# A transformer block on one core: the attention stage's order of work, written out in the kernel instead of searched for while building

## The chip, the cores and the metric

The kernel runs on one core of one Trainium2 chip. The metric is device time in microseconds (us); the median of three runs of the kernel before is 2465.46 us (2460.82 to 2471.02). A profile of one further execution, which took 2466.89 us, is read below.

The engines are named as the profile names them: PE (TensorE, matmuls; PEld are its weight loads), DVE (VectorE), ACT (ScalarE), POOL (GpSimd) and SP (SyncE, which issues nearly all DMAs). Each runs its own list of instructions in the order in which the kernel was built.

## The reference

```python
mod = (silu(c) @ w_mod).reshape(1, 6, 1, -1)
sa, ca, ga, sb, cb, gb = (mod[:, i] for i in range(6))
h = layernorm(x) * (1 + ca) + sa
x = x + ga * attention(h, wqkv, wo)        # 32 heads of 18, softmax(q k^T / sqrt(18)) v, then @ wo
h = layernorm(x) * (1 + cb) + sb
x = x + gb * (silu(h @ w1) @ w2)           # 576 -> 4608 -> 576
return x
```

The sequence has 2048 rows of 576 numbers, in float32. Matmuls are done in a reduced float32 form, with operands split into a high and a low part, so that one product of the reference is two or three products here.

## The kernel before, in words

The rows are four blocks of 512 queries. Attention is done block by block, and in each block for eight quads of four heads. The work beside it differs: beside the first block's attention run the remaining q and k projections, beside that of block b + 1 the output projection and the whole MLP of block b. The last block's projection and MLP come alone at the end. So the program has a start (projections, up to about 156 us), four attention stages, here stage 0 to stage 3, and a tail from about 2192 us.

In a stage PE is given five kinds of work, in an order that one list fixes:

- **A slot** ("s" in the list, function `slots`, L311): two matmuls of half the array's height, one of scores (`psa`, L978), whose row maximum DVE takes (`mx`, L980), and one of scores once more, transposed (`psb`, L1061), whose exponential ACT takes (`pt`, L1063). `psb` has two PSUM banks, `psa` three in stage 0 and two later. There are 2048 slots; the scores for the maximum run 38 pairs of slots ahead of the others.
- **A unit** (a digit n stands for n units, function `values`, L374): eight matmul rows in the profile, `psv` at L1071, which multiply a finished piece of `pt` with the values. The array is used in another tiling here (quarters by columns), so that going in and out is a change of mode.
- **A filler item** ("f", function `item`, L441): the next piece of the projections or the MLP, mostly two or three pairs of half-height matmuls at L734. Items come in a fixed sequence, `FILL`.
- **A turn** is a place inside a group of such items: the halves of the array swap their two PSUM banks. PE's next matmul waits there for a small ACT instruction (L741), which itself waits for the last matmul of the first halves. ACT works in order, so that it comes behind the exponentials.
- **Rows** ("x", function `rows`): short full-height transposes at a quad's end (`pst`, `pso`).

Each PE step is followed by work of other engines. Where these instructions and the DMA issues on SP stand in their lists is decided by `Sim`, a model of the core inside the kernel: it keeps a clock per engine, and pushes each following instruction when the model says that its input is there. So the list of PE steps also fixes the order on ACT, DVE, POOL and SP.

Before the change the list comes from `search` (L519), a beam search over this model at build time. It keeps 24 states per level and 4 units in a row at most; `choices` (L489) lets the filler run at most 24 slots ahead of or behind an even pace, holds a quad's rows back until they are due, and adds a unit only when its exponentials are within 200 of the model's nanoseconds of being done. The list found is then played once more, with instructions emitted (L1868 to L1877):

```python
    order, best = sim.search()
    sim = Sim(FILL, ENDS, LOADS)
    sim.hT = HT
    with tc.manual_schedule():
        sim.real = Emit()
        sim.skip()
        for what in order:
            assert sim.act(what)
```

What is left of `FILL` when the list ends is emitted ahead of the last block's tail.

Of the kernel before, what the change touches and what calls it, by code (L numbers as in the profile page):

```python
# [31 lines left out]
NQUAD = H // 4  # L32
# [16 lines left out]
EML = 4  # L49
GB = 6  # L50
MB = 4
END = -4
END0 = 40
LP0 = 1000
LP = 8000
PB = 10
# [13 lines left out]
MOVE = {"k": 4 * 608, "q": 4 * 608, "v": 2300, "m": 320, "raw": 645, "w": 1700, "ws": 1480, "x": 780, "qk": 1640, "rawqk": 1280}  # L70
COLD = 3000
SWITCH = {("half", "values"): 115, ("values", "half"): 250, ("half", "full"): 195, ("full", "half"): 95, ("full", "values"): 95, ("values", "full"): 143}
RUN = 4
ROWS = 1400
AHEAD = 24
BEAM = 24
GRAIN = 300
PHI = 60
ACT_, DVE_, GPS_, SP_ = range(4)


def f(ap):
# [30 lines left out]
class Sim:  # L113


    def __init__(self, fill, ends, loads):
        self.fill, self.ends, self.loads = fill, ends + ends[-1:], loads
        self.sums = [sum(it.cost for it in fill[a:b]) for a, b in zip([0] + ends, ends)] + [1]
        self.real = None
        self.t = self.n = self.w = self.dma = 0  # L120
        self.mode = "half"
        self.free = [0] * 4
        self.queue = [[] for _ in range(4)]
        self.rings = {"f": [0] * 2, "a": [0] * 3, "b": [0] * 2, "v": [0]}
        self.head = {"f": 0, "a": 0, "b": 0, "v": 0}
        self.keys = {k: 0 for k in [("mr", 0), ("Q", 0), ("Q", 1), ("V", 0), ("kb", 0)] + [("ka", n) for n in range(6)]}
        self.held = {}
        self.exps = {}
        self.now = 2 * LEAD
        self.total = NQB * NQUAD * 32  # L130
        self.p = 0
        self.pend = []
        self.later = []
        self.pos = 0
        self.done = 0
        self.span = 2 * LEAD, NQUAD * 64 - END0
        self.block = 0
        self.path = None

    def clone(self):  # L140
        s = Sim.__new__(Sim)
        s.__dict__.update(self.__dict__)
        s.free = self.free[:]
        s.queue = [q[:] for q in self.queue]
        s.rings = {k: v[:] for k, v in self.rings.items()}
        s.head = dict(self.head)
        s.keys = dict(self.keys)
        s.held = dict(self.held)
        s.exps = dict(self.exps)
        s.pend = self.pend[:]  # L150
        s.later = self.later[:]
        return s

    def push(self, chain, i, ready):
        self.n += 1
# [114 lines left out]
    def key(self, k):  # L270
        return self.keys.get(k)

    def ahead(self):
        if self.pos >= self.ends[self.block]:
            return 0
        a, n = self.span
        return self.now - (a + n * self.done / self.sums[self.block])

    def more(self):
        return self.now < 2 * (self.total + LEAD)  # L280

    def over(self):
        return not (self.more() or self.pend or self.later)

    def skip(self):

        while self.pos < self.ends[self.block]:
            it = self.fill[self.pos]
            if it.cost and it.fn is not None:
                return True  # L290
            if it.keys:
                if any(self.keys.get(k) is None for k in it.keys):
                    return True
            if it.opens and not self.reopen():
                return False
            self.pos += 1
            self.done += it.cost
            if self.real and it.fn:
                it.fn()
            for delay, chain in it.chains:  # L300
                self.push(chain, 0, self.t + delay)
            self.set(it.sets, self.t)
        return True
# [112 lines left out]
    def rows(self):  # L416

        _, _, kind, i = self.later[0]
        key = ("ms", i) if kind == "m" else ("ov", i)
        at, rel = self.known(lambda: self.key(key)), self.known(lambda: self.when("a"))  # L420
        if at is None or rel is None:
            return False
        b, qd = divmod(i, NQUAD)
        self.later.pop(0)
        rel = max(at, rel)
        slot = ("r", "a", self.take("a")[0])
        if kind == "m":
            self.work(110, "full", rel)
            e = self.real.max_b(i) if self.real else (None, None)
            self.push((Op(DVE_, 270, e[0], (slot,)), Op(SP_, ROWS, e[1], (("k", ("mr", i)),), MOVE["m"])), 0, self.t + 150)  # L430
            return True
        self.work(440, "full", rel)
        e = self.real.out_b(i) if self.real else (None,) * 6
        chain = [Op(DVE_, 252, e[0])] + [Op(DVE_, 225, e[1 + n], (slot,) if n == NST - 1 else ()) for n in range(NST)]
        if qd == NQUAD - 1:
            chain.append(Op(GPS_, 650, e[5], (("k", ("post", b)),)))
            self.block = b + 1
            self.done = 0
            self.span = self.now, NQUAD * 64 - END
        self.push(tuple(chain), 0, self.t + 150)  # L440
        return True  # L441

    def item(self):
# [21 lines left out]
            self.push(chain, 0, self.t + delay)  # L465
        self.set(it.sets, self.t + 500)
        self.pos += 1
        self.done += it.cost
        return True

    def act(self, what):
        ok = {"s": self.slots, "f": self.item, "x": self.rows}[what]() if what != "v" and not isinstance(what, int) else self.values(what)
        return ok and self.skip()

    def ready(self):

        n = 0
        for kid in self.pend[:RUN]:
            c, at = self.exps.get(kid, (0, 0))
            if kid[0] != self.pend[0][0] or c < 4 or at > self.t + 200:  # L480
                break
            n += 1
        return n

    def choices(self):
        self.advance()
        work = self.pos < self.ends[self.block]
        ahead = self.ahead()
        out = []  # L489
        if self.later:  # L490
            due, last = self.later[0][:2]
            can = self.can_rows()
            if can and self.now >= last:
                return ["x"]
            if can and (self.now >= due or not self.more()):
                out.append("x")
            if not can and self.now >= last:
                return ["f"]
        n = self.ready()
        if n:  # L500
            out.append(n)
        elif self.pend and (not self.more() or self.p >= PB):
            out.append(1)
        room = self.p + (self.now % 2 == 0) <= PB
        if self.more() and room and (ahead < AHEAD or not work):
            out.append("s")
        if work and (ahead > -AHEAD or not self.more()):
            out.append("f")
        if not out:
            out = ["f"] if work else ["s"]  # L510
        return out

    def search(self):

        self.skip()
        levels = {0: [self]}
        heap = [0]
        best = None
        while heap:  # L519
            lv = heappop(heap)  # L520
            states = levels.pop(lv)
            states.sort(key=lambda s: s.t + PHI * len(s.pend))
            seen, kept = {}, 0
            for s in states:
                sig = s.now, s.pos, len(s.pend), len(s.later)
                if seen.get(sig, 0) >= 2:
                    continue
                seen[sig] = seen.get(sig, 0) + 1
                kept += 1
                if kept > BEAM:  # L530
                    break
                if s.over():
                    rest = sum(it.cost for it in self.fill[s.pos:])
                    if best is None or s.t + rest < best[0]:
                        best = s.t + rest, s
                    continue
                made = []
                for what in s.choices() + [None]:
                    if what is None:
                        if made or s.pos >= s.ends[s.block]:  # L540
                            break
                        what = "f"
                    c = s.clone()
                    if c.act(what):
                        c.path = s.path, what
                        made.append(c)
                for c in made:
                    k = c.w // GRAIN
                    if k not in levels:
                        levels[k] = []  # L550
                        heappush(heap, k)
                    levels[k].append(c)
        out, p = [], best[1].path
        while p:
            out.append(p[1])
            p = p[0]
        return out[::-1], best


class Task:  # L560
# [96 lines left out]
def tile_adaln_block(ctx: ExitStack, tc: tile.TileContext, x, wqkv, wo, w1, w2, c, wfirst, wcol, out):  # L657
# [1209 lines left out]

    sim = Sim(FILL, ENDS, LOADS)  # L1868
    sim.hT = HT
    order, best = sim.search()  # L1870
    sim = Sim(FILL, ENDS, LOADS)
    sim.hT = HT
    with tc.manual_schedule():
        sim.real = Emit()
        sim.skip()
        for what in order:
            assert sim.act(what)  # L1877
        sim.t = 10 ** 9
        sim.advance()
    state["tail"] = True  # L1880
# [53 lines left out]
```

## Time and profile before

| | |
|---|---|
| median of three runs | 2465.46 us |
| profiled execution | 2466.89 us |
| its span, first to last instruction | 2465.1 us |
| PE busy | 2391.9 us, 97% |
| DVE busy | 1777.0 us, 72% |
| ACT busy | 1491.2 us, 60% |
| POOL busy | 581.9 us, 24% |
| mean granted TensorE clock | 0.991 |

Times in the trace are counted from the span's start. "Busy" of PE runs to the end of each matmul as modelled, and matmuls overlap, so that two halves that run side by side show about 0.39 us each while the next pair begins 0.23 us after them. What PE achieves is therefore read from the distance between starts. A row of waits says how long an engine was idle before the instructions named, and whose end released it.

### The profile page before, as it was taken

How to read it: one execution, taken by the hardware profiler on the slowest of the kernel's cores; microseconds unless marked ns; L12 is line 12 of the kernel's file. 1: busy time of each engine (PE TensorE's matmuls, PEld its weight loads, DVE VectorE, ACT ScalarE, POOL GpSimd, SP SyncE). 2: the span in 40 equal slices, each digit the busy share in tenths (PEclk: the TensorE clock that was granted, in tenths of full speed). 3: DMA queues.
4: the chain of work that ended last, by engine and by line, in shares of the span. 5: the costliest groups of instructions: out<-in, count | busy, mean ns of one | idle time of the engine just before them, and what ended most of it. 6: DMA issues, size and time to landing. Idle time of an engine off the chain costs nothing.

```text
span 2465.1 us, 52723 instructions
## 1 busy us (share of the span) xinstructions
PE 2391.9 (97%) x20528; PEld 1632.2 (66%) x20528; DVE 1777.0 (72%) x3180; ACT 1491.2 (60%) x2712; POOL 581.9 (24%) x729
## 2 busy tenths in 40 slices
PE   5999999999999999999999999999999999999999
PEld 4875544543666666665676666776767667678998
DVE  7877887887877777777777777778777777424333
ACT  4236776776667666666567677676667777742121
POOL 4213332303333434344311111111211111110000
PEclk9999999998999999999999999999999999999999
DMA  7857777745445556555455544454535554436563
GB/s 245 255 194 234 250 252 225 250 151 190 156 161 182 172 159 210 171 176 167 161 176 176 180 152 154 157 188 158 197 136 195 178 177 151 138 111 241 180 216 118
DMA packets 210296, 452.29 MB, mean 183 GB/s; under 512 B 22594, under 2 KB 78306, under 8 KB 210050
## 3 DMA queue, kind: packets, MB, share of 16 engines
q1 hardware_dynamic: 210050, 448.93, 54.8%
q8 instruction: 164, 2.69, 0.5%
q14 instruction: 82, 0.67, 0.1%
HBM read 362.51 MB, written 85.80 MB: 182 GB/s over the span
## 4 chain that ended last, share of the span: by engine, by line
PE 88%; DMA 4%; DVE 4%; ACT 1%; POOL 1%; issue 1%; SPq 0%; ACTq 0%; POOLq 0%; DVEq 0%
PE ps L734 28%; PE psv L1071 18%; PE psa L978 12%; PE ps L728 10%; PE psb L1061 9%; PE psqk L734 4%; DVE mx L980 2%; PE psp L734 2%; PE psv L734 1%; PE pso L1078 1%; DMA kt<-kscr 1%; PE psp L728 1%; DMA w1raw<-in_w 1%; ACT pt L1063 1%; DMA xt<-in_x 1%
## 5 line engine op out<-in xcount | busy, mean ns | idle before, releaser
L980 DVE TENSOR_REDUCE mx<-psa 128x1 f32<-128x512 f32 x2048 | 1345.3, 686 | 380.2 <-PE psb L1061 215.8
L1063 ACT ACTIVATE pt<-psb 128x512 f32<-128x512 f32 x2048 | 1166.6, 598 | 587.1 <-PE psb L1061 350.0
L1061 PE MATMUL psb<-qt,kt 56*128 56x512 f32 x2048 | 810.3, 429 | 10.8 <-ACT pt L1063 10.8
L978 PE MATMUL psa<-kt,qt 54*128 54x512 f32 x2048 | 763.3, 417 | 18.3 <-DVE mx L980 11.7
L978 PEld LDWEIGHTS psa<-kt,qt 54*128 54x128 f32 x2048 | 360.2, 186 | 267.3 <-DVE mx L980 152.0
L1071 PE MATMUL psv<-pt,vt 128*32 128x512 f32 x4096 | 514.4, 608 | 0.3
L734 PEld LDWEIGHTS ps<-w2t,g 64*128 64x128 f32 x4992 | 384.9, 185 | 75.1 <-issue 41.9
L734 PE MATMUL ps<-w2t,g 64*128 64x288 f32 x4992 | 427.1, 297 | 2.4 <-DVE x L1254 1.2
L1061 PEld LDWEIGHTS psb<-qt,kt 56*128 56x128 f32 x2048 | 363.7, 186 | 66.3 <-ACT pt L1063 54.5
L734 PE MATMUL ps<-hh,w1t 64*128 64x512 f32 x2160 | 381.5, 399 | 0.1
L734 PEld LDWEIGHTS ps<-hh,w1t 64*128 64x128 f32 x2160 | 209.2, 186 | 63.0 <-issue 13.9
L1399 POOL TENSOR_TENSOR g<-etmp,g 128x512 fp32r<-128x512 f32 x108 | 138.0, 1296 | 475.2 <-ACT g L1395 458.1
L1071 PEld LDWEIGHTS psv<-pt,vt 128*32 128x32 f32 x4096 | 101.9, 109 | 200.3 <-issue 189.8
L1261 POOL TENSOR_TENSOR x<-x,gt 128x288 f32<-128x288 f32 x116 | 93.0, 802 | 544.3 <-ACT gt L1257 528.1
L734 PE MATMUL ps<-hl,w1t 64*128 64x512 f32 x864 | 176.5, 391 | 0.0
L1254 DVE TENSOR_TENSOR x<-ps,x 128x288 f32<-128x288 f32 x184 | 83.4, 454 | 101.6 <-PE ps L728 70.7
L728 PE MATMUL ps<-w2t,g 128*128 128x288 f32 x960 | 130.1, 295 | 1.4 <-ACT g L1395 0.9
L728 PEld LDWEIGHTS ps<-w2t,g 128*128 128x128 f32 x960 | 128.6, 188 | 2.8 <-ACT g L1395 1.2
L1388 ACT ACTIVATE eq<-ps 128x512 f32<-128x512 f32 x36 | 21.6, 600 | 146.3 <-PE ps L728 146.3
L728 PE MATMUL ps<-hh,w1t 128*128 128x512 f32 x360 | 106.9, 390 | 0.5 <-DVE hh L708 0.5
L734 PEld LDWEIGHTS ps<-hl,w1t 64*128 64x128 f32 x864 | 87.0, 186 | 16.1
L1391 DVE SCALAR_TENSOR_TENSOR etmp<-etmp 128x512 f32<-128x512 f32 x108 | 73.1, 710 | 15.9 <-ACT etmp L1388 15.9
(134 smaller groups left out, 2074.3 us busy)
## 6 DMA issues: line engine op xcount, KB each, us to landing
kt<-kscr SPq DMA_DIRECT2D x1024, 108.0 KB
w1t<-w1s SPq DMA_DIRECT2D x144, 640.0 KB
w2t<-w2s SPq DMA_DIRECT2D x108, 576.0 KB
w1s<-w1out SPq DMA_DIRECT2D x72, 320.0 KB
w2s<-w2t SPq DMA_DIRECT2D x36, 576.0 KB
vt<-vscr SPq DMA_DIRECT2D x32, 608.0 KB
qt<-qscr SPq DMA_DIRECT2D x128, 108.0 KB
w1raw<-in_w SPq DMA_DIRECT2D x72, 160.0 KB
```

The costliest lines, as they stand in the source:

```text
L728: mm(self.ps[late], lhsT=lhsT, rhs=rhs, start=(i == 0), stop=(i == self.n - 1))
L734: done = mm(self.ps[g], lhsT=lhsT[rows], rhs=rhs[rows], start=(s == 0), stop=(s == 2 * self.n - 1))
L978: mm(ps, lhsT=t["q"][64 * j:64 * j + 54, hp, stt * P:(stt + 1) * P], rhs=t["k", kc, hp][64 * j:64 * j + 54, :], start=True, stop=True)
L980: return lambda: nc.vector.tensor_reduce(t["mx"][:, 2 * j + hp, stt, kc:kc + 1], ps, axis=AX.X, op=ALU.max)
L1061: mm(ps, lhsT=t["kb", kt // 4, hp][64 * e:64 * e + 56, kt % 4 * P:(kt % 4 + 1) * P], rhs=t["q"][64 * e:64 * e + 56, hp, :], start=True, st ...
L1063: return lambda: nc.scalar.activation(t["P"][kt, hp][:, e, :], ps, AF.Exp, scale=SCALE)
L1071: mm(t["ps"][32 * h:32 * h + 32, :], lhsT=t["v"][:, c0:c0 + 32], rhs=t["P"][kt, h // 2][:, h % 2, :], start=(kt == 0), stop=(kt == NKT - 1 ...
L1078: nc.tensor.transpose(ps[:, s4, :], ov[:, s4 * P:(s4 + 1) * P], ident)
L1254: nc.vector.tensor_add(c["x1", j][:, hs], ps, c["x1", j][:, hs])
L1261: nc.gpsimd.tensor_add(c["x1", j][:, HH:], c["x1", j][:, HH:], box.pop("gt"))
L1391: nc.vector.scalar_tensor_tensor(d["t"], d["t"], 1.0, d["u"], op0=ALU.add, op1=ALU.mult)
L1399: (nc.vector if last else nc.gpsimd).tensor_tensor(gt[:, 1, :], d["t"], f(gt[:, 0, :]), op=ALU.subtract)
```

## The change

The kernel now holds the list itself: a string `ORDER` of 4472 characters, played through the same `Sim` with the same filler items. The search, its limits and its constants are gone. The model's durations, the buffers, the instructions and what each computes are the same. One line of the string (stage 0) and the end of the program:

```diff
-    sim = Sim(FILL, ENDS, LOADS)
-    sim.hT = HT
-    order, best = sim.search()
     sim = Sim(FILL, ENDS, LOADS)
     sim.hT = HT
     with tc.manual_schedule():
         sim.real = Emit()
         sim.skip()
-        for what in order:
-            assert sim.act(what)
+        for what in ORDER:
+            assert sim.act(int(what) if what.isdigit() else what)
...
+ORDER = (
+    "ssffsfsffsfsfssfsfsfsfsfsfsfs11ss1ss1sfsfsfsfsfsfsfssfsfsfssfsfsffss2ss1ss1ss1ss1ssfsfsfssfsfss1ss1xss1ss1sfssfssfssfsfs"
...
-    def search(self):
...
-    def choices(self):
...
-    def clone(self):
```

Because lines were removed, line numbers differ by 82 in what follows: L896 is the old L978 (`psa`), L979 the old L1061 (`psb`), L989 the old L1071 (`psv`), L652 the old L734 (half-height pairs), L646 the old L728 (full height) and L996 the old L1078 (`pso`).

First place: PE in stage 0, from the slot with the number 82 of the list on (of 2048). Before:

```order
L978 MATMUL psa_3058<-kt5_82,qt_2307 128x512
L1061 MATMUL psb_3060<-qt_1486,kt7_84 128x512
L978 MATMUL psa_3066<-kt5_82,qt_2307 128x512
L1061 MATMUL psb_3068<-qt_1486,kt7_84 128x512
L978 MATMUL psa_3078<-kt0_77,qt_2307 128x512
L1061 MATMUL psb_3080<-qt_1486,kt6_83 128x512
L978 MATMUL psa_3085<-kt0_77,qt_2307 128x512
L1061 MATMUL psb_3087<-qt_1486,kt6_83 128x512
L1071 MATMUL psv2_2902<-pt0_2083,vt1_2094 32x512 x2
L1071 MATMUL psv2_2902<-pt1_2084,vt1_2094 32x512 x2
L978 MATMUL psa_3104<-kt0_77,qt_2307 128x512
L1061 MATMUL psb_3106<-qt_1486,kt7_84 128x512
```

Now, from slot 84 on:

```order
L896 MATMUL psa_3071<-kt0_77,qt_2311 128x512
L979 MATMUL psb_3073<-qt_1486,kt6_83 128x512
L896 MATMUL psa_3081<-kt0_77,qt_2311 128x512
L979 MATMUL psb_3083<-qt_1486,kt6_83 128x512
L989 MATMUL psv2_3047<-pt6_2089,vt1_2094 32x512 x2
L989 MATMUL psv2_3047<-pt7_2090,vt1_2094 32x512 x2
L896 MATMUL psa_3097<-kt0_77,qt_2311 128x512
L979 MATMUL psb_3099<-qt_1486,kt7_84 128x512
L896 MATMUL psa_3101<-kt0_77,qt_2311 128x512
L979 MATMUL psb_3103<-qt_1486,kt7_84 128x512
```

Four slots stood in a row before the next unit (two rows of `psv` here are one unit); now a unit stands after every second slot.

Second place: PE in stage 2, the turn in the middle of an MLP group (the same group in both; `ps1` are its two banks, `hh` and `hl` its input, `w1t` its weights). Before:

```order
L734 MATMUL ps1_19696<-hh_16956,w1t_19509 128x512
L734 MATMUL ps1_19697<-hh_16956,w1t_19519 128x512
L978 MATMUL psa_19771<-kt1_78,qt_19123 128x512
L1061 MATMUL psb_19773<-qt_17072,kt6_83 128x512
L734 MATMUL ps1_19696<-hh_16956,w1t_19509 128x512
L734 MATMUL ps1_19697<-hh_16956,w1t_19519 128x512
```

Now:

```order
L652 MATMUL ps1_19882<-hh_17038,w1t_19722 128x512
L652 MATMUL ps1_19883<-hh_17038,w1t_19726 128x512
L896 MATMUL psa_19961<-kt5_82,qt_18969 128x512
L979 MATMUL psb_19963<-qt_18012,kt7_84 128x512
L896 MATMUL psa_19966<-kt0_77,qt_18969 128x512
L979 MATMUL psb_19968<-qt_18012,kt6_83 128x512
L652 MATMUL ps1_19882<-hh_17038,w1t_19722 128x512
L652 MATMUL ps1_19883<-hh_17038,w1t_19726 128x512
```

Between the last matmul of the first halves and the first after the turn stood one slot; now two stand there.

Third place: PE at the end of stage 3, after the last slot. Before, the last unit and what follows it:

```order
L1071 MATMUL psv2_30986<-pt1_2084,vt1_2094 32x512 x2
L1071 MATMUL psv2_30986<-pt2_2085,vt1_2094 32x512 x2
L1071 MATMUL psv2_30986<-pt3_2086,vt1_2094 32x512 x2
L1078 MATMUL pso_31474<-ident_85,ov_31472 128x128 x4
L1239 MATMUL psT_31490<-ident_85,ot_25037 128x128 x4
```

Now:

```order
L989 MATMUL psv2_30742<-pt1_2084,vt1_2094 32x512 x2
L989 MATMUL psv2_30742<-pt2_2085,vt1_2094 32x512 x2
L989 MATMUL psv2_30742<-pt3_2086,vt1_2094 32x512 x2
L652 MATMUL ps1_31380<-hh_24938,w1t_30925 128x512
L652 MATMUL ps1_31381<-hh_24938,w1t_30939 128x512
```

The last MLP group of block 2 (28 pairs) now follows the last unit: four pairs, the transposes `pso`, then its other 24 pairs and only then the transposes `psT` of the tail.

More of the change, by code (lines that the diff above doesn't have):

```diff
@@ L51 @@
 MB = 4
-END = -4
-END0 = 40
 LP0 = 1000
@@ L117, in __init__ @@
         self.fill, self.ends, self.loads = fill, ends + ends[-1:], loads
-        self.sums = [sum(it.cost for it in fill[a:b]) for a, b in zip([0] + ends, ends)] + [1]
         self.real = None
@@ L134, in __init__ @@
         self.pos = 0
-        self.done = 0
-        self.span = 2 * LEAD, NQUAD * 64 - END0
         self.block = 0
-        self.path = None
-    def clone(self):
[L141 to L152, printed above, removed]
     def push(self, chain, i, ready):
@@ L271, in key @@
         return self.keys.get(k)
[L273 to L277, printed above, removed]
     def more(self):
         return self.now < 2 * (self.total + LEAD)
-    def over(self):
-        return not (self.more() or self.pend or self.later)
     def skip(self):
@@ L296, in skip @@
             self.pos += 1
-            self.done += it.cost
             if self.real and it.fn:
@@ L437, in rows @@
             self.block = b + 1
-            self.done = 0
-            self.span = self.now, NQUAD * 64 - END
         self.push(tuple(chain), 0, self.t + 150)
@@ L467, in item @@
         self.pos += 1
-        self.done += it.cost
         return True
@@ L473, in act @@
         return ok and self.skip()
[L475 to L483, printed above, removed]
-    def choices(self):
[L486 to L511, printed above, removed]
@@ L513, in search @@
-    def search(self):
[L515 to L557, printed above, removed]
```

43 lines of the change are left out of this document (38 added, 5 removed).

## The prediction

> **What bounds the kernel now.** I read the page first, then the stages, then PE's starts in the timeline, then the waits.
>
> ```profile
> span 2465.1 us, 52723 instructions
> PE 2391.9 (97%) x20528; PEld 1632.2 (66%) x20528; DVE 1777.0 (72%) x3180; ACT 1491.2 (60%) x2712; POOL 581.9 (24%) x729
> PE 88%; DMA 4%; DVE 4%; ACT 1%; POOL 1%; issue 1%; SPq 0%; ACTq 0%; POOLq 0%; DVEq 0%
> ```
>
> PE sets the end: 88% of the chain. That leaves open whether it works or stands during its busy time. The stages, with both ends (stages 0 to 3, then the tail):
>
> ```profile
> 156.00:602.00 446.00, 430.66 (x2821) 215.91 (x2819) 357.40 (x626) 309.98 (x573) 118.54 (x171) 0.96 0.70 223
> 602.00:1149.00 547.00, 532.95 (x4909) 348.80 (x4908) 415.73 (x720) 360.75 (x659) 224.36 (x297) 0.99 0.52 170
> 1149.00:1677.00 528.00, 523.49 (x5063) 359.13 (x5061) 409.34 (x719) 359.27 (x654) 101.16 (x108) 1.00 0.52 174
> 1677.00:2192.00 515.00, 513.88 (x4991) 355.76 (x4987) 359.81 (x637) 357.56 (x655) 86.06 (x88) 1.00 0.47 160
> 2192.00:2465.00 273.00, 264.30 (x1628) 241.46 (x1620) 108.81 (x214) 51.16 (x83) 8.15 (x13) 1.00 0.51 182
> ```
>
> The columns are window, length, busy time of PE, PEld, DVE, ACT, POOL, granted clock, DMA share, GB/s. The four stages last 2036 us, and only there does the order change. What PE's steps cost when nothing holds them is read from starts, here in stage 2:
>
> ```profile
> 1401.82 0.39 PE L978 MATMUL psa<-kt,qt 54*128 54x512 f32 x1
> 1402.16 3.64 PE L1071 MATMUL psv<-pt,vt 128*32 128x512 f32 x32
> 1405.73 0.49 PE L978 MATMUL psa<-kt,qt 54*128 54x512 f32 x1
> 1406.08 0.39 PE L978 MATMUL psa<-kt,qt 54*128 54x512 f32 x1
> 1411.22 0.39 PE L734 MATMUL ps<-hl,w1t 64*128 64x512 f32 x2
> 1411.45 0.62 PE L734 MATMUL ps<-hh,w1t 64*128 64x512 f32 x4
> 1411.91 0.39 PE L978 MATMUL psa<-kt,qt 54*128 54x512 f32 x1
> 1412.18 0.73 PE L734 MATMUL ps<-hh,w1t 64*128 64x512 f32 x4
> 1412.75 0.39 PE L978 MATMUL psa<-kt,qt 54*128 54x512 f32 x1
> 1043.22 2.71 PE psv L1071 x24
> 1510.44 3.57 PE psv L1071 x32
> ```
>
> A pair 512 wide takes 0.23 us (1411.22, 1411.45, and two pairs to 1411.91); so does a slot. A unit takes 3.57 - 2.71 = 0.86 us (the last two rows, pieces of the chain with four and three units). By width a pair of 288 takes 0.13. A visit to the units costs more than its units: 0.11 going in (1401.82 to 1402.16, less 0.23), 3.57 - 4 x 0.86 = 0.13 inside, 0.12 on the first slot back (1405.73 to 1406.08): 0.36, so 0.18 a change of mode.
>
> The old order has in its stages 2048 slots (473 us), 1848 pairs of 512 (427), 2832 pairs of 288 (377), 512 units (438) and some 32 us of transposes: 1747 us of work. The stages last 2036. So **289 us of PE's apparently busy time are not work**, and the change can touch nothing else. By stage: 130, 75, 49, 33.
>
> 764 changes of mode at 0.18 are 138 of them. The rest is waiting, and this is how it looks in a run of slots in stage 0:
>
> ```profile
> 571.47 0.49 PE L978 MATMUL psa<-kt,qt 54*128 54x512 f32 x1 [0.54 <-DVE mx L980]
> 572.06 0.50 PE L978 MATMUL psa<-kt,qt 54*128 54x512 f32 x1
> 572.74 0.49 PE L978 MATMUL psa<-kt,qt 54*128 54x512 f32 x1 [0.17 <-DVE mx L980]
> 573.35 0.75 PE L978 MATMUL psa<-kt,qt 54*128 54x512 f32 x1
> ```
>
> Slots 0.6 to 0.7 us apart instead of 0.23: PE is shown busy for 0.49 of each 0.6, though it works 0.23. The followers set that pace:
>
> ```profile
> L980 DVE TENSOR_REDUCE mx<-psa 128x1 f32<-128x512 f32 x2048 | 1345.3, 686 | 380.2 <-PE psb L1061 215.8
> L1063 ACT ACTIVATE pt<-psb 128x512 f32<-128x512 f32 x2048 | 1166.6, 598 | 587.1 <-PE psb L1061 350.0
> L1061 PE MATMUL psb<-qt,kt 56*128 56x512 f32 x2048 | 810.3, 429 | 10.8 <-ACT pt L1063 10.8
> L978 PEld LDWEIGHTS psa<-kt,qt 54*128 54x128 f32 x2048 | 360.2, 186 | 267.3 <-DVE mx L980 152.0
> PEld psa L978 <- DVE mx L980: 152.0, 238, 1.5
> PEld psb L1061 <- ACT pt L1063: 54.5, 165, 3.5
> PEld ps L734 <- ACTq L741: 20.5, 72, 0.8
> ```
>
> With two banks, slot k cannot begin before the exponential of slot k - 2 is out: 0.43 + 0.60 + 0.19 for the load is 1.22 us after that slot's start. So two slots go at PE's pace, and every further one in a row at ACT's or DVE's. The weight loads waited 206 us for these two, an upper bound of what slots lose.
>
> **The change part by part.** No instruction is added or removed.
>
> *Slot waits.* Runs of three or more slots in a row: 47 in the old order, 12 in the new one; slots beyond the second of a run: 102 and 29. Slots also come too soon with little between them, so I laid both orders out with the prices above: each step at its price, each slot pushed until the exponential two slots back (1.22 us) and the maximum three back in stage 0, two later (0.42 + 0.69 + 0.19) are done, exponentials following one another at 0.60 and maxima at 0.69. The pushes sum, by stage, to 73, 29, 11 and 11 us before, and 45, 13, 9 and 6 now: 124.7 against 73.3, **-51 us**. Check: with the changes of mode the old order comes to 263 of the 289 that the trace has. Other work on ACT and DVE is left out of this, so bounds are half of it (-26) and the share of over-long runs that go, 73 of 102, taken of all 125 (-89).
>
> *Changes of mode.* 764 become 743: 21 x 0.18 = **-4**, between 0 and -6.
>
> *Turns.* 83 of 182 turns had one slot inside, 3 have now; the others two. With one, the old order loses 0.04 + 0.11 at 1411.91 to 1412.75 (0.27 and 0.57 against 0.23 and 0.46): 80 x 0.15 = 12. The loads waited 20.5 in 72 such waits, the upper end; the lower is 0, if two slots are no cover either. I take **-15**, nearer to the example.
>
> *The clock.* Where slots and units stand alone, the grant halves, though PE shows busy:
>
> ```profile
> 232.00:242.00 10.00, 10.00 (x36) 4.29 (x38) 5.97 (x10) 4.56 (x9) 2.18 (x3) 0.50 0.85 281
> 573.00:587.00 14.00, 13.18 (x49) 3.81 (x47) 8.42 (x16) 6.17 (x12) 6.05 (x9) 0.51 0.57 180
> 416.32 1.28 PE L1061 MATMUL psb<-qt,kt 56*128 56x512 f32 x2 [3.08 <-ACT pt L1063]
> 417.00:424.00 7.00, 7.00 (x33) 2.71 (x33) 3.98 (x8) 3.30 (x6) 1.32 (x3) 0.55 0.93 262
> ```
>
> By the stage rows the lost grant is 0.04 x 446 + 0.01 x 547 = 23 us, most of it inside waits already counted. What the count leaves unexplained, 289 - 263 = 26 less some 15 for turns, is 11; as 7 in 10 of the over-long runs go, **-8**, between 0 and -16.
>
> The Trainium skill ("TensorE: Matmul & The Clock Gate", section "What's actually happening") has the rate halve after an idle window of about 3.4 us; by that only the third row, behind a stop of 3.08 us, would follow, and this term would be about -3 (half of 7 us). The same page, section "A second HAM failure mode: psum-queue depth-cycling", has PE's short stops between groups suffice, and by that the whole 23 us hang on the order. The first two rows, 24 us at half rate with PE shown busy for 23 of them, agree with the second section.
>
> *Other waits of items*, such as the 3.08 us above (PE stopped behind ACT), lie at other places in the new order: -2, between -10 and +10.
>
> *The tail.* 24 pairs move behind the last unit: 5.5 us of the same work, no change. They cover the wait for `ov` at the stage's end, but `ps2`, which reads what this group makes, follows 2.5 us after it, and the chain copy, tanh, product, cast, subtraction (0.6 + 0.6 + 0.71 + 0.6 + 1.3 by the rows below) needs 3.8.
>
> ```profile
> 2193.19 0.66 PE L1078 MATMUL pso<-ident,ov 128*128 128x128 f32 x4 [0.72 <-ACT ov L1043]
> 2193.68 2.35 PE L1239 MATMUL psT<-ident,ot 128*128 128x128 f32 x20
> L1391 DVE SCALAR_TENSOR_TENSOR etmp<-etmp 128x512 f32<-128x512 f32 x108 | 73.1, 710 | 15.9 <-ACT etmp L1388 15.9
> L1399 POOL TENSOR_TENSOR g<-etmp,g 128x512 fp32r<-128x512 f32 x108 | 138.0, 1296 | 475.2 <-ACT g L1395 458.1
> ```
>
> So -0.7 and about +1.5: **+1**.
>
> Sum: -51 - 4 - 15 - 8 - 2 + 1 = **-79 us**. The profiled execution spans 2465.1 (2466.89 with what lies around it), so its span becomes 2386; the median of the runs, 2465.5, becomes **2386 us**, 3.2% less.
>
> **The rivals.**
>
> *PE has no more to give.* The page shows PE 97% busy. Read literally, 2465.1 - 2391.9 = 73 us are idle, 35 of them in the four stages (15, 14, 5 and 1). If all of those go, and nothing else does, 2430. A milder form is that each wait moves to another engine (DVE has 357 of 446 us in stage 0), so that half the slot term and half the turns come: -26 - 8 - 4 = -38, 2427. For it: the order was laid out with a model, and the kernel's other work on ACT and DVE isn't in my count. Against it: the 289 us. The Trainium skill ("Trainium Kernel Development and Optimization", section "Performance Expectations") calls matmul busy time a bad metric since matmuls are pipelined; the starts 0.6 us apart agree.
>
> *More than forecast.* All ends: -89 - 6 - 20 - 16 would be 2334; half way there, 2360. For it: the counts of long runs and short turns fall by much more than four in ten.
>
> *ACT stands behind late loads.* In stage 0 ACT converts nine pieces of weights, each behind its own load, and the exponentials queue behind it:
>
> ```profile
> 415.05 0.74 ACT L785 ACTIVATE wqh<-raw 128x640 fp32r<-128x640 f32 x1 [4.00 <-DMA raw<-in_wqkv]
> ACT wqh L785 <- DMA raw<-in_wqkv: 15.5, 4, 10.7
> ```
>
> If a denser stage 0 (DMA share 0.70 already) makes loads late, all nine could be held as long as the longest, 10.7 us: +96, so 2482. From 9 us each it decides the sign. Against it: the old order shows 15.5 us in four such waits, start included.
>
> *The order does nothing* beyond changing places of waits: 2465. Against it stand 83 turns that become 3.
>
> **How the numbers follow.** Forecast 0.68 (own range 2366 to 2404), less (2427) 0.15, more (2360) 0.10, nothing 0.04, late loads 0.03. A measurement of this kernel can tell about 0.5%, 12 us, from no change. So faster 0.93, same 0.04, slower 0.03. The range takes in most of "more" and part of "less": 2360 to 2422.
>
> **What would show it.** Right: the loads' waits for `mx` and `pt` fall from 206 us to about 120, those for L741 from 20.5 to under 6; PE's rows in stage 0 stand closer, its stage takes about 410 us; fewer half-rate stretches. Stages 0 and 1 give some 50 of the 79. Wrong: the waits fall and the span doesn't, or waits for `wqh`, `kt` or `g` appear in PE's and ACT's rows that the old trace hasn't.

## The result and the profile after

The changed kernel takes **2389.3 us** (median of four runs, 2388.66 to 2393.49) against 2466.5 us for the kernel before (four runs, 2460.82 to 2471.02). The ratio is 0.9692, with a 95% interval from 0.9668 to 0.9715: 77 us less. The forecast was 2386. The page of the changed kernel, its span, busy times and chain:

```profile
span 2391.7 us, 52731 instructions
PE 2336.2 (98%) x20528; PEld 1635.2 (68%) x20528; DVE 1782.0 (75%) x3179; ACT 1487.1 (62%) x2711; POOL 584.7 (24%) x729
PE 88%; DVE 5%; DMA 3%; POOL 2%; issue 2%; ACT 1%; SPq 0%; ACTq 0%; POOLq 0%; DVEq 0%
```

The matmuls are the same 20528, and yet PE's busy time falls from 2391.9 to 2336.2. So 56 of the 73 us between these two executions (spans of 2465.1 and 2391.7) were gained inside time in which PE is shown busy. The stages (window, length, busy time of PE, PEld, DVE, ACT, POOL, granted clock, DMA share, GB/s):

```profile
156.00:566.00 410.00, 403.22 (x2804) 205.11 (x2800) 356.27 (x622) 308.01 (x569) 114.96 (x167) 0.99 0.73 236
566.00:1099.00 533.00, 526.37 (x4957) 357.83 (x4956) 426.97 (x735) 369.60 (x674) 230.67 (x301) 1.00 0.55 180
1099.00:1617.00 518.00, 516.35 (x5079) 363.88 (x5079) 412.87 (x725) 359.77 (x658) 98.72 (x106) 1.00 0.53 175
1617.00:2111.00 494.00, 491.83 (x4887) 350.54 (x4887) 349.89 (x616) 344.26 (x635) 87.92 (x90) 1.00 0.50 164
2111.00:2392.00 281.00, 271.79 (x1680) 246.58 (x1676) 110.09 (x216) 53.09 (x87) 8.72 (x13) 1.00 0.52 182
```

Stage 0 has gone from 446 to 410 us, the stages 1 to 3 from 547, 528 and 515 to 533, 518 and 494; the tail has grown from 273 to 281, mostly by the moved work (28 pairs, 6.4 us). The stages cannot be compared by length alone, since filler items moved from one to another. With each stage's own steps at the prices of the prediction, what is not work was 130, 75, 49 and 33 us and is now some 96, 56, 37 and 24: **34, 19, 12 and 9 us less**. The check is the sum: the stages are 81 us shorter together, 6.4 of it is moved work, and 75 remain.

What a denser stage 0 looks like, from PE's starts in the timeline of the changed kernel:

```profile
243.85 0.50 PE L896 MATMUL psa<-kt,qt 54*128 54x512 f32 x1
243.86 0.73 PE L979 MATMUL psb<-qt,kt 56*128 56x512 f32 x2
244.20 0.40 PE L896 MATMUL psa<-kt,qt 54*128 54x512 f32 x1
244.53 1.07 PE L989 MATMUL psv<-pt,vt 128*32 128x512 f32 x8
245.52 0.50 PE L896 MATMUL psa<-kt,qt 54*128 54x512 f32 x1
```

Two slots and a unit, and the next slot 1.67 us after the first (243.85 to 245.52). The work is 2 x 0.23 + 0.86 = 1.32, the visit to the units 0.36: 1.68. Nothing is waited for: in these 1.67 us ACT gets through two exponentials (2 x 0.60) and DVE through two maxima (2 x 0.69).

A turn with two slots inside, in stage 2 of the changed kernel:

```profile
1402.35 0.39 PE L979 MATMUL psb<-qt,kt 56*128 56x512 f32 x1
1402.36 0.62 PE L896 MATMUL psa<-kt,qt 54*128 54x512 f32 x2
1402.59 0.39 PE L979 MATMUL psb<-qt,kt 56*128 56x512 f32 x1
1402.81 0.64 PE L652 MATMUL ps<-hh,w1t 64*128 64x512 f32 x4
1403.28 0.40 PE L652 MATMUL ps<-hl,w1t 64*128 64x512 f32 x2
```

Slots and pairs follow at 0.23 apiece, where the old one-slot turn had a gap behind the slot and another between the pairs. The loads' waits, from the view of waits:

```profile
PEld psa L896 <- DVE mx L898: 141.3, 208, 1.5
PEld psb L979 <- ACT pt L981: 28.8, 109, 2.6
PEld ps L652 <- ACTq L659: 1.5, 5, 0.5
```

The turns' waits are gone (20.5 us to 1.5), those for `pt` are halved (54.5 to 28.8), and those for `mx` have hardly moved (152.0 to 141.3). Together the loads wait 170 us for the followers instead of 206. And the clock, first in the windows that ran at half rate before, then in the three that do so now:

```profile
232.00:242.00 10.00, 10.00 (x72) 6.94 (x70) 9.44 (x16) 8.42 (x16) 3.52 (x5) 1.00 0.81 255
573.00:587.00 14.00, 13.76 (x141) 9.75 (x136) 11.22 (x21) 8.05 (x16) 8.21 (x14) 1.00 0.54 182
416.00:424.00 8.00, 8.00 (x58) 5.67 (x54) 7.91 (x15) 7.15 (x14) 1.84 (x3) 1.00 0.92 308
160.00:163.40 3.40, 3.02 (x14) 2.48 (x16) 0.69 (x1) 2.64 (x5) 0.97 (x3) 0.56 0.71 216
362.00:365.40 3.40, 3.27 (x16) 2.87 (x17) 1.19 (x2) 1.68 (x3) 1.32 (x2) 0.53 0.84 254
771.00:774.40 3.40, 3.40 (x17) 1.08 (x19) 1.36 (x2) 1.08 (x2) 3.40 (x4) 0.56 0.71 205
```

Half-rate stretches inside the stages sum to 10 us, where they were 44. Two places stand for what a new order may cost. PE stops once for 1.77 us behind a load of `kt`, where its two such stops in the old order were 0.9 us together. In the new tail it stops three times behind the moved pairs; the old tail had a stop of 0.72 us behind `ov` and the same 0.26 behind `tl`:

```profile
362.13 0.76 PE L979 MATMUL psb<-qt,kt 56*128 56x512 f32 x1 [1.77 <-DMA kt<-kscr]
...
2120.54 1.53 PE L1157 MATMUL psT<-ident,ot 128*128 128x128 f32 x12 [0.38 <-DVE etmp L1309]
2122.34 1.73 PE L646 MATMUL ps<-w2t,g 128*128 128x288 f32 x11 [0.26 <-DVE tl L1165]
2124.40 2.00 PE L646 MATMUL ps<-w2t,g 128*128 128x288 f32 x13 [0.33 <-POOL g L1317]
```

ACT's long wait of 4.00 us for a piece of weights is not there any more; of all such waits only the one at the program's start is left, 10.8 us.

### The profile page after: what moved, and what is told of

The parts are those of the page before. It is cut to its first block, busy times and chain, and to the rows that moved or that the text cites. A ratio compares the mean times of both kernels' runs of the same rounds, so it can differ in the third digit from the quotient of the medians.

```text
span 2391.7 us, 52731 instructions
## 1 busy us (share of the span) xinstructions
PE 2336.2 (98%) x20528; PEld 1635.2 (68%) x20528; DVE 1782.0 (75%) x3179; ACT 1487.1 (62%) x2711; POOL 584.7 (24%) x729
## 4 chain that ended last, share of the span: by engine, by line
PE 88%; DVE 5%; DMA 3%; POOL 2%; issue 2%; ACT 1%; SPq 0%; ACTq 0%; POOLq 0%; DVEq 0%
PE ps L652 27%; PE psv L989 18%; PE psa L896 13%; PE psb L979 10%; PE ps L646 10%; PE psqk L652 4%; DVE mx L898 2%; PE psv L652 1%; PE psp L652 1%; PE pso L996 1%; DMA raw<-in_w 1%; PE psp L646 1%; DMA kt<-kscr 0%; POOL raw L1069 0%; POOL w2t L1075 0%
## 5 line engine op out<-in xcount | busy, mean ns | idle before, releaser
L979 PE MATMUL psb<-qt,kt 56*128 56x512 f32 x2048 | 803.2, 426 | 4.6 <-ACT pt L981 2.4
L896 PE MATMUL psa<-kt,qt 54*128 54x512 f32 x2048 | 753.5, 414 | 8.7 <-DVE mx L898 5.2
L896 PEld LDWEIGHTS psa<-kt,qt 54*128 54x128 f32 x2048 | 358.2, 185 | 258.3 <-DVE mx L898 141.3
L989 PE MATMUL psv<-pt,vt 128*32 128x512 f32 x4096 | 505.1, 601 | 0.0
L652 PE MATMUL ps<-w2t,g 64*128 64x288 f32 x4992 | 423.5, 294 | 3.2 <-POOL w2t L1075 1.6
L652 PEld LDWEIGHTS ps<-w2t,g 64*128 64x128 f32 x4992 | 390.1, 185 | 43.1 <-issue 12.7
L979 PEld LDWEIGHTS psb<-qt,kt 56*128 56x128 f32 x2048 | 363.1, 184 | 44.2 <-ACT pt L981 28.8
L652 PE MATMUL ps<-hh,w1t 64*128 64x512 f32 x2160 | 379.0, 393 | 0.1
L989 PEld LDWEIGHTS psv<-pt,vt 128*32 128x32 f32 x4096 | 102.4, 109 | 213.0 <-issue 205.6
L652 PEld LDWEIGHTS ps<-hh,w1t 64*128 64x128 f32 x2160 | 216.0, 186 | 40.2 <-issue 4.7
L652 PE MATMUL ps<-hl,w1t 64*128 64x512 f32 x864 | 177.9, 391 | 0.0
L646 PE MATMUL ps<-w2t,g 128*128 128x288 f32 x960 | 130.4, 296 | 1.7 <-ACT g L1313 0.9
L646 PEld LDWEIGHTS ps<-w2t,g 128*128 128x128 f32 x960 | 128.6, 188 | 3.3 <-ACT g L1313 1.2
L646 PE MATMUL ps<-hh,w1t 128*128 128x512 f32 x360 | 106.9, 390 | 0.5 <-DVE hh L626 0.5
L652 PEld LDWEIGHTS ps<-hl,w1t 64*128 64x128 f32 x864 | 88.4, 186 | 13.9
L1025 POOL CAST w1out<-w1raw 128x320 fp32r<-128x320 f32 x72 | 32.4, 450 | 215.0 <-DMA w1raw<-in_w 189.7
```

The lines of the kernel that those rows point to most:

```text
L646: mm(self.ps[late], lhsT=lhsT, rhs=rhs, start=(i == 0), stop=(i == self.n - 1))
L652: done = mm(self.ps[g], lhsT=lhsT[rows], rhs=rhs[rows], start=(s == 0), stop=(s == 2 * self.n - 1))
L896: mm(ps, lhsT=t["q"][64 * j:64 * j + 54, hp, stt * P:(stt + 1) * P], rhs=t["k", kc, hp][64 * j:64 * j + 54, :], start=True, stop=True)
L979: mm(ps, lhsT=t["kb", kt // 4, hp][64 * e:64 * e + 56, kt % 4 * P:(kt % 4 + 1) * P], rhs=t["q"][64 * e:64 * e + 56, hp, :], start=True, st ...
L989: mm(t["ps"][32 * h:32 * h + 32, :], lhsT=t["v"][:, c0:c0 + 32], rhs=t["P"][kt, h // 2][:, h % 2, :], start=(kt == 0), stop=(kt == NKT - 1 ...
L1025: nc.gpsimd.tensor_copy(d["out"][:, 1], d["raw"])
```

## The experiments

The question is no longer whether the order helps, but which of the terms did it: fewer slots in a row, turns with two slots, the clock, or something that only a search sees. Each kernel is the changed one with another string; the instructions and what they compute are the same. In their traces the lines behind the string are one higher (L897 is `psa`, L980 `psb`, L990 `psv`, L653 the pairs, L660 the turn).

### The changed kernel again

> The changed kernel once more, as the measure for the runs beside it. Expected 2389 us within 4. Half-rate stretches: the old order's trace has 44 us of half clock inside the stages, the new one's 10 (160, 362 and 771 us). If the order sets them, this execution shows about 10 us again, at those places; if they come by chance, another sum (20 us or more) at other places with the same time.

Measured: 2389.7 us (2386.5 to 2390.7), ratio 0.9678 (0.9661 to 0.9695). Two half-rate stretches, at 554 and 769 us, 6.8 us together. The places are not those of the execution above, and the sum is about as small, so neither of the two outcomes came out whole. What follows: where the clock halves differs from one execution to the next, but how much of it there is goes with the order: the granted clock is 0.998 or 0.999 in all eight runs of this kernel, and 0.988 to 0.994 in the thirteen of the kernel before that were timed beside it.

### One slot inside each turn

In 172 turns the second slot goes behind the next item:

```diff
-    "...ffsfsffsfsfssfsfsfsfs...
+    "...ffsfsffsfsfsfssfsfsfs...
```

> The new order, with the second slot of 172 of its turns moved behind the turn's first item. The number of slots, units and mode changes stays, and by the count of the prediction slot waits too (69 us against 71). Theory, turns cost what the prediction took (0.15 us each): 172 x 0.15 = +26, 2415 us. By the mean that the starts of the old trace give (0.195 us lost per turn with one slot, 0.069 with two): 172 x 0.126 = +22, 2411. Rival, a turn's wait is covered by what PE has in flight: 2389. The loads' waits for L741's place rise to about 172 x 0.28 = 49 us by the theory.

Measured: 2409.3 us (2407.1 to 2413.5), ratio 0.976 (0.9738 to 0.9783), 19.6 us more than the changed kernel again: **0.114 us for a turn**. The wait view and one of the turns in the timeline:

```profile
PEld ps L653 <- ACTq L660: 39.3, 157, 0.5
```

```profile
1409.16 0.39 PE L980 MATMUL psb<-qt,kt 56*128 56x512 f32 x1
1409.16 0.39 PE L897 MATMUL psa<-kt,qt 54*128 54x512 f32 x1
1409.43 0.73 PE L653 MATMUL ps<-hh,w1t 64*128 64x512 f32 x4
1409.99 0.39 PE L980 MATMUL psb<-qt,kt 56*128 56x512 f32 x1
```

The slot takes 0.27 to the next start instead of 0.23, and two pairs take 0.56 instead of 0.46. The loads wait 39.3 us, the time rises by 19.6: half of it. By the starts, a turn with two slots still loses some 0.07 to 0.1 us, an estimate that depends on where a turn is taken to end. The prediction had taken it as free. If a turn is worth the same in the old order, eighty were worth 80 x 0.114 = 9 us.

### Four slots in a row

At 48 places of stage 0, two slots, a unit, two slots, a unit become four slots and two units:

```diff
-    "...fsfsfs11ss1ss1sfsfsf...
+    "...fsfsfs11ssss11sfsfsf...
```

> The new order, with slot-slot-unit-slot-slot made slot-slot-slot-slot-unit at 48 places of stage 0. By the count of the prediction slot waits rise by 50 us, and 76 mode changes fewer at 0.18 give back 14: +36, 2425 us. Rival, ACT and DVE average over a few slots and only their sums count: the 14 us come and the waits don't: 2375. On the clock: if short stops suffice, half-rate stretches in stage 0 rise from 3 to over 20 us, and the time by up to 10 more; if it takes an idle window of 3.4 us, they stay at 3.

Measured: 2422.4 us (2420.1 to 2424.1), ratio 0.9812 (0.9795 to 0.9829), 33 us more. One of the places:

```profile
251.27 0.50 PE L897 MATMUL psa<-kt,qt 54*128 54x512 f32 x1
251.28 0.49 PE L980 MATMUL psb<-qt,kt 56*128 56x512 f32 x1
251.61 0.40 PE L897 MATMUL psa<-kt,qt 54*128 54x512 f32 x1
251.61 0.39 PE L980 MATMUL psb<-qt,kt 56*128 56x512 f32 x1
251.85 0.40 PE L897 MATMUL psa<-kt,qt 54*128 54x512 f32 x1
252.49 0.50 PE L980 MATMUL psb<-qt,kt 56*128 56x512 f32 x1 [0.25 <-ACT pt L982]
252.83 0.39 PE L897 MATMUL psa<-kt,qt 54*128 54x512 f32 x1
252.98 0.49 PE L980 MATMUL psb<-qt,kt 56*128 56x512 f32 x1
253.40 1.93 PE L990 MATMUL psv<-pt,vt 128*32 128x512 f32 x16
255.26 0.50 PE L897 MATMUL psa<-kt,qt 54*128 54x512 f32 x1
```

The third slot's `psb` begins at 252.49, 1.22 us after the first slot (251.27), which is the rule of two banks to the hundredth. The whole place takes 3.99 us, where the changed kernel takes 2 x 1.67 = 3.34 for the same steps: 0.65 more, and 48 x 0.65 = 31 of the 33 us. By the starts of both traces all 48 places together take 194 us instead of 159. On the clock, more than 20 us at half rate in stage 0, the outcome by which short stops suffice, did not come: 13.7 us run at half rate in the whole execution, none of them right behind one of the 48 places (the stretch at 586 us follows a run of six slots that the changed kernel has too). And the loads:

```profile
PEld psa L897 <- DVE mx L899: 92.8, 153, 1.5
PEld psb L980 <- ACT pt L982: 65.0, 188, 2.6
```

They wait 158 us, less than the 170 of the changed kernel, in a program that is 33 us slower. So the idle time of the weight loads is not what PE loses.

### Two slots inside the old order's turns

The other way round: in the old order the next slot is pulled ahead into 82 turns, and nothing else is changed.

```diff
-    "...1fssffffsffsfffsfsfffss...
+    "...1fssffffsffssffffsfffss...
```

> The old order, with a second slot pulled ahead into 82 of its 83 one-slot turns; nothing else moved. Turns alone by the prediction: 82 x 0.15 = -12, so 2454 us; by the starts -10, 2456. But the slot pulled ahead now stands close to the one before it, and by the count slot waits rise from 123 to 139 us: +16. Together +4 to +6, 2471. The first would say that the turn alone was worth its term, the second that a turn gains only if the slots around it are spaced again.

Measured: 2473.1 us over ten runs (2467.6 to 2485.2), ratio 1.0032 (1.0013 to 1.005), 7 us **more** than before. That two slots in a turn are good by themselves falls; the count had it a few us slower, since the slot that is pulled ahead now stands close to the one before it. The turns' own waits did go, from 20.5 us to 1.8, and the loads' waits for `mx` rose from 152.0:

```profile
PEld psa L897 <- DVE mx L899: 172.1, 284, 1.7
```

The profiled execution has 68 us at half rate instead of 44 (granted clock 0.986). But the clock is not what took back the turns' gain: one line through these ten runs and the thirteen of the kernel before, with -1.7 us for each 0.001 of granted clock, leaves the ten 6.7 us slower at the same clock (standard error 1.0). That the slots did it is what the count says; no run shows it by itself.

### The new order in stage 0 alone

Stage 0 as in the changed kernel; from there on the old narrow search decides:

```diff
     "...(stage 0 of the changed kernel)...
-    "...fssffsffss1fssfffssfffssf11fsf...
+    "...sss1ssfssffsffs11fssfffss1sfsf...
```

> The new order for stage 0, then the old narrow search, started from the state that this leaves, for stages 1 to 3 and the rest. By the count of the prediction against the old order: slot waits 98 for 123 us (-25), 790 mode changes for 764 (+5), 87 one-slot turns for 83: -20, so 2446 us. By the stages of the two traces, stage 0 alone took 446 us before and 410 now: -36, so 2430, if nothing of it is taken back later. Rival, an early stage 0 makes later stages wait for loads or weights: above 2450.

Measured: 2430.6 us (2428.3 to 2431.5), ratio 0.9854 (0.9831 to 0.9877): 34 us less than the kernel before timed beside it (2464.5). Its first two stages:

```profile
156.00:566.00 410.00, 403.96 (x2802) 205.83 (x2798) 356.03 (x622) 307.90 (x569) 115.77 (x167) 0.99 0.73 237
566.00:1110.00 544.00, 532.12 (x4904) 345.75 (x4902) 415.67 (x721) 360.10 (x659) 226.80 (x300) 1.00 0.52 174
```

Stage 0 takes the new 410 us, stage 1 nearly the old 547. The gain is the 34 us by which stage 0's time without work had fallen, so the reading by stages adds up. The count of pushes and mode changes alone asked for -20 us; it is 14 short, in the stage which has most of the old order's lost clock. The mean granted clock of these runs is 0.9965 against 0.992 of the kernel before, some 7 of the 14 at 1.5 us per 0.001 (last section). The other half is not assigned.

### A wider search of the old kind

The string is what the old search finds when it keeps 96 states per level instead of 24, with everything else as it was:

```diff
-    "ssffsfsffsfsfssfsfsfsfsfsfsfs11ss1ss1sf...
+    "ssssssfssfs1ss1ssffss1ssffsfsfss1ss1ssf...
```

> The old search with 96 states kept per level for 24, nothing else. Its list has 32 over-long runs for 47, slot waits 99.5 for 123 us by the count (-23), 743 mode changes (-4), 95 one-slot turns for 83 (+2): -25, so 2441 us. Rival, a wider search finds orders that look better only on paper: 2455 to 2466.

Measured: 2436.1 us (2431.9 to 2444.8), ratio 0.9882 (0.985 to 0.9915): 28 us less than before, 37% of what the change gives. The count asked for 25, and the rival by which a wider search gains only on paper falls. So part of the gain was within reach of the old search itself.

### Searching on

Two orders come from a search that starts at the changed kernel's string and moves steps by a few places. One goes by the kernel's model as it is; the other by the mean over three versions of the model in which one delay each is made longer (the way from one engine to the next, the overlap of following instructions on ACT and DVE, the landing of loads), so that a step should not stand just at the edge.

By the model as it is:

```diff
-    "ssffsfsffsfsfssfsfsfsfsfsfsfs11ss1ss1sfsf...
+    "sfsffsfsfsfsfssfsfsfsfsfsffss11ss1ss1ssff...
```

> The same local search from the new order for the same reason of length, with the kernel's model as it is, without margins. By the count: slot waits 65 for 71 us (-5), 748 mode changes (+1), 9 one-slot turns (+1): -3, so 2386 us. If margins are what matters, this gains much less than the order with margins (under 6 us, 2384 or above); if any further search does it, both gain alike.

With lengthened delays:

```diff
-    "ssffsfsffsfsfssfsfsfsfsfsfsfs11ss1ss1sfsf...
+    "sfsffsfsfsfsfssfsfsfsfsfsfsfs11ss1ss1ssff...
```

> The new order with some 1500 of 4575 steps moved by a few places, found by a local search from the new order; what it lowers is the mean over the kernel's model with three delays made longer in turn (hops between engines, the overlap of ACT's and DVE's instructions, DMA landing). By the count of the prediction: slot waits 62 for 71 us (-8), 768 mode changes for 743 (+4.5), 14 one-slot turns for 3 (+1.4): -2, so 2387 us. Rival theory: a list that stands on the edge of each wait loses wherever the chip is a little later than planned, which the count doesn't see, and margins are worth 10 to 20 us: 2370 to 2379.

Measured: 2382.4 us (2380.4 to 2385.4), ratio 0.9664 (0.9637 to 0.9691), by the model as it is; 2387.3 us (2383.5 to 2391.6), ratio 0.968 (0.9654 to 0.9707), with lengthened delays. The second is about the changed kernel's time, as the count said; the theory that the new order's remaining waits come from steps standing too near the edge (2370 to 2379) falls, as far as these three delays go. The first is 7 us below the changed kernel, and 3 by the two ratios to the kernel before. The intervals of the two ratios overlap, but none of its four runs is as slow as the fastest of the changed kernel's eight (2386.5).

Searched further from there, with steps moved by up to 40 places:

```diff
-    "ssffsfsffsfsfssfsfsfsfsfsfsfs11ss1ss1sfsf...
+    "sffssffsfsfsfssfsfsfsfsfsfsfs11ss1ss1sfsf...
```

> The order of order_same_model, searched on without margins, with moves over up to 40 steps. By the count: slot waits 64 for 65 us, 746 mode changes for 748: -2 against that run's 2382, so 2380 us. If what is left to a reordering is used up, it is the same 2382 within 3.

Measured: 2382.1 us over five runs (2378.1 to 2383.7), ratio 0.9659 (0.9637 to 0.9681). Its page:

```profile
span 2377.9 us, 52742 instructions
PE 2327.6 (98%) x20528; PEld 1623.6 (68%) x20528; DVE 1779.6 (75%) x3179; ACT 1488.4 (63%) x2711; POOL 583.2 (25%) x729
```

The longer search gives nothing more. As far as these searches reach, moving steps about under this model is used up 82 us below the old order (2464.1 beside these runs). These two strings are the best versions found.

### Eight slots in a row

The clock had hardly answered to runs of four. So at 12 places of stage 0 eight slots stand in a row, with their four units behind them:

```diff
-    "...sffss11ss1ss1ss1ss1ssfsf...
+    "...sffss11ssssssss1111ssfsf...
```

> The new order, with four pairs of slots and the three units between them made eight slots in a row and then the three units, at 12 places of stage 0. By the count of the prediction: slot waits 102 for 71 us (+31), 675 mode changes for 743 (-12): +19, so 2408 us. The runs are for the clock. In the traces so far the clock halves after a stretch of 3.4 us in which PE's priced work is about 0.4 of the time or less, idle gap or not; runs of four with units around them stay above that (0.59), so their clock stayed at 0.998. Eight slots 0.65 us apart are 5.2 us at 0.23 / 0.65 = 0.36. If the share of work decides, about half of the 12 runs halve the clock for 3.4 us each: granted clock 0.994 or less, and at 1.5 us per 0.001 (fast runs of the old order) another +6, 2414 us. If an idle window of 3.4 us is needed, the clock stays at 0.998 and the time at 2408.

Measured: 2417.4 us (2416.2 to 2419.3), ratio 0.9805 (0.9784 to 0.9827), 28 us more than the changed kernel. The granted clock is 0.992 in the profiled execution and up to 0.994 in the others, and nine stretches, 37 us in all, run at half rate. Seven of the nine begin 3 to 5 us after the start of one of the 12 runs of eight. Stage 0 (the row goes some 20 us into stage 1) and one of the places, with the run of slots first and then what follows it:

```profile
156.00:617.00 461.00, 451.51 (x2981) 235.49 (x2982) 370.51 (x653) 322.18 (x595) 127.10 (x185) 0.96 0.69 221
189.40:192.80 3.40, 3.15 (x16) 1.68 (x13) 3.36 (x7) 2.45 (x6) 0.31 (x1) 1.00 0.92 344
193.00:199.00 6.00, 6.00 (x29) 1.97 (x31) 2.16 (x4) 1.94 (x4) 1.32 (x2) 0.50 1.00 352
```

In the first stretch PE is shown busy for 3.15 of 3.40 us. Twelve half-height matmuls begin in it, at half of 0.23 apiece 1.4 us of work, and no start is more than 0.7 us behind the one before. Then the grant halves. The theory that only a longer stop of PE does that expected 2408 us at a clock of 0.998; the one by which slots at the followers' pace suffice expected 2414. The latter is nearer, in time and clock. It is 3 us short too; it reckoned with a clock of 0.994, and the mean of the four runs is 0.993.

## Why the prediction was right

| term | predicted | by the runs | from |
|---|---|---|---|
| slot waits | -51 | -48 | four in a row cost 33, and 14 more that fewer changes of mode gave back: 47 where the count says 50, so 0.94 x 51 |
| changes of mode | -4 | -4 | not tested by itself |
| turns | -15 | -9 | 0.114 x 80 |
| clock | -8 | -10 | mean grant 0.9918 to 0.9985, at 1.5 us per 0.001 (last section) |
| other waits of items | -2 | -7 | what is left over |
| tail | +1 | +1 | tail 7.6 us longer, of it 6.4 moved work |
| sum | -79 | -77 | |

That the sum comes within 2 us is partly luck: slots and turns were put 9 us too high, the clock and the other waits 7 us too low. And the column in the middle adds up only because its fifth row is a remainder.

**That 289 us of busy time were not work** was the step on which all else stood. It held: 75 of them are gone with the same matmuls. The rival by which PE has no more to give fell at this. Of the 35 us that PE was shown idle in the four stages 17 are left; the other gains lie under "busy".

**The slot term** carried most of the sum and was right in kind. The rule behind it is seen directly: third slot 1.22 us after the first. For runs of four in stage 0 the count was within a tenth in size; that the same factor holds for the pushes elsewhere is taken over, not shown.

**The turns were mis-sized.** The step read one turn with one slot, took its 0.15 us as all gained (12 us), and went up to 15 towards the loads' 20.5. A turn with two slots is not free either. The difference is 0.114 us by the run, -9 instead of -15, and the loads' 20.5 us was no price.

**The clock's term** came out near, by a price that is read from the scatter between runs and not from an edit of the clock alone, and the Trainium skill's two rules can be told apart a little. By "TensorE: Matmul & The Clock Gate", section "What's actually happening", a window of about 3.4 us without work halves the rate; in the run with eight slots in a row no such window precedes the stretch at 193 us, and the stop of 1.77 us in the changed kernel, at whose end at 362 us the rate is already halved, is shorter too. The section "A second HAM failure mode: psum-queue depth-cycling" of the same page, on short stops between groups, agrees with the rows. It gives no threshold; four slots in a row weren't enough at 48 places, eight were at 7 of 12.

**The other waits** were put at -2 between -10 and +10; what is left over for them is -7. Some are seen: the 3.08 us stop of PE behind ACT at 416 us is gone (that window now runs at full rate). But the rest was not assigned by a run, and the errors of the other terms are in it.

**One reading was wrong.** The loads' waits for `mx` and `pt` were to fall from 206 to about 120 us and fell to 170. The runs show why it was no test: with four slots in a row they fell further, to 158, and the time rose by 33 us. The prediction used the 206 us as an upper bound of what slots lose, which is not contradicted; as a gauge of the gain it fails. The other readings held: turn waits under 6 (1.5), stage 0 at 410, stages 0 and 1 with 53 of the gain against some 50, less half rate. Of what would have spoken against it, PE's wait behind `kt` grew from 0.9 us to 1.8, and ACT waits once for 3.5 us behind the same loads; both weigh little.

**The tail** came out as forecast, though the prediction counts 24 moved pairs (5.5 us) where all 28 of the group follow the last unit (6.4 us). It changes nothing in the sum, since the last stage loses what the tail gains.

**Late loads** did not come. DMA share in stage 0 rose from 0.70 to 0.73, and ACT's waits for weights shrank.

What stays: some 214 us in the stages are still not work. By the count 134 of them are 743 changes of mode and 71 to 73 are slot waits. That the orders found by searching on end at 2382 says that these searches don't reach them by order alone.

## What to carry to other kernels

Price steps by the distance between starts where nothing holds them, multiply by their number, and compare with the stage: a row that says 97% busy hid 289 us. Where a ring of two buffers paces an engine, two steps in a row are free and a third waits for the follower, so something else belongs between; here another order under the same model gained 3%, and a wider search of the old kind a third of that, where the one edit by hand of the old order made it 7 us slower. Take neither the idle time of weight loads nor a wait total as the price of a cause; take the difference that a run with that one cause shows.

## What the hardware showed that was not expected

**Half rate without a stop.** Over the before, after and eight-in-a-row executions, the half-rate stretches come in multiples of 3.4 us, and what precedes each is a stretch of that length in which the steps that begin, at their prices, are mostly some 0.3 to 0.5 of the time (before: 0.27, 0.41, 0.41, 0.52, 0.37, 0.46, and once 0.03; after: 0.34, 0.37 and 0.22; eight in a row: 0.34 to 0.5). The longest distance between two starts in it is often short: 0.94 us ahead of 573 us in the kernel before, 0.37 ahead of 319 us with eight in a row. Stretches with shares of 0.37 to 0.47 that did not halve exist too, so this is no sharp edge; what decides inside it is open.

**The scatter of the runs goes with the clock.** Thirteen runs of the kernel before, timed together, range from 2458.6 us to 2472.7, at granted clocks of 0.994 to 0.988: -1.85 us for each 0.001, correlation -0.83. Over 20 runs of it, it is -1.5 (-0.86), and over 29, -1.4 (-0.83); over the ten runs of the old order with two-slot turns, 2467.6 at 0.994 to 2485.2 at 0.985, it is -1.6 (-0.93). A thousandth of the span is 2.47 us. That less than this is lost fits PE standing behind its followers for part of the slow time, which no run here separates.
